# A relu-squared attention with a mixture of adapters behind it: the loads of A and B are planned behind q and k of the fourth and fifth quads

## The chip, the cores and the metric

The kernel runs on one core of one Trainium2 chip. The metric is the device time of one execution in microseconds; lower is better. Times are given as the median of several runs, and one execution is profiled.

## The reference

Eight batches of twelve heads, 448 positions, head size 64. The attention has no softmax: the scores are clipped at zero and squared. Its output, 3584 rows of 768, goes through a gate that picks two of eight adapters of rank 16 for each row and adds what they give.

```python
scores = scale * np.matmul(q, k.transpose(0, 1, 3, 2))
attn = np.maximum(scores, 0.0) ** 2 / S
x = np.matmul(attn, v)            # then (B*S, H*D) = (3584, 768)
logits = x @ w_gate               # the two largest of 8 are kept
w = exp(sel - max); w /= w.sum()
for e in range(8):                # rows that picked e
    delta[mask] += w[mask] * ((x[mask] @ A[e]) @ B[e])
out = x + delta
```

q, k, v are float32 of 8x12x448x64; A is 8x768x16, B is 8x16x768.

## The kernel before

**Tiles.** Four heads of one batch are loaded together; this is called a quad here, and there are 24 (eight batches `b` with three quads `c` each), numbered from 0. One load of a quad's q, k or v is two DMAs from POOL (`load`, L337 to L355; L342 is its line in the profile), one for each half of the 128 partitions, and it casts float32 to bf16 on the way. The rings hold three quads of q, three of k and six of v. q of the first quad comes another way (SP and ACT), its k in two pieces (L362).

**Stages.** For a quad, TensorE transposes q and k (`tp`, 56 small matmuls, L496), and VectorE copies the result to `qkT` (L509). Then come seven steps `j`, each with a step index `n` that runs through the kernel: `qk` (L545, four matmuls into two PSUM banks), `relu` on ACT (L569; for the first seven steps VectorE may do it, L571), the square on VectorE for two steps at once (L588), and `pv` (L606). After seven steps the result is copied to `xt` (L629). Behind the attention, groups of three tiles of 128 rows go through the gate (L647 to L704), a transpose of the weighted z (L730, L744), and each tile then gets its output: x by an identity matmul (L761), the adapters' second product with `B_sb` in two groups of eight matmuls (L781), two copies out of PSUM (L805) and the stores from SP (L825).

**A, B and sel.** `a_raw` and `g_raw` hold A and the gate's weights as loaded by `aw_fn` (L404, L408). `sel`, made on POOL by a memset and a select (L392, L393), is the 0/1 matrix with which TensorE puts A's rows in order (`aw_place`, L424, 72 matmuls, copied at L434 to `awg`). The gate reads `awg`. `b_fn` (L412) loads B twice, once to each half of the partitions.

**Order.** Nothing is ordered by hand. Every piece of work is an `Op` with the engines it may run on, a duration and a latency in us, the pieces it depends on, and a rank. `schedule` (L68) plays them through on a clock of its own, gives each engine the ready piece with the smallest rank, and the program is then issued in the order of the planned starts. On the chip, each engine follows this fixed order and waits where data is missing; a planned dependency that stands for no data is no wait there. A load has duration 0.63 for each half and latency 2.5; users see it 0.05 later. Its rank is the number of the quad, plus 1.2 for v. `sel_op` and `a_load` have rank 3.5, `b_load` 4.5. The first loads (`first_load`) have no dependencies; a later load depends on the transposes of the quad three before, and from some point on it really waits for a given relu (`pace`). On TensorE, `pick` (L123) takes the smallest rank with a surcharge for changing the matmul mode, but turns to the next `qk` when the piece chosen would outlast what ACT still has before it:

```python
cover = max(free["ACT"], t) + sum(o.dur["ACT"] for o in relus)
if q and t + best.dur[e] + 0.1 * (best.mode != mode) + 0.1 * (best.mode != "64") + 0.4 > cover + SLACK:
    return q[0]
```

At most three pairs of PSUM banks may hold scores at a time (`SCAP`).

The functions that the diff touches:

Of the kernel before, what the change touches and what calls it, by code (L numbers as in the profile page):

```python
# [14 lines left out]
J = 7  # L15
# [18 lines left out]
E_O0 = 1  # L34
E_O1 = 0
E_Z = 1
SYNC = mybir.DependencyInfo(mybir.DependencyClass.Sync, mybir.DependencyReason.DATA)
LEAD = -10
LSTEP = 2.0
# [8 lines left out]
class Op:  # L48
    def __init__(
        self, engs, dur, lat, fn, deps=(), after=None, mode=None, kind="", take=(), give=(), rank=0.0,  # L50
        banks=None, free=(),
    ):
        self.engs, self.fn = engs, fn
        self.dur = dur if isinstance(dur, dict) else dict.fromkeys(engs, dur)
        self.lat = lat if isinstance(lat, dict) else dict.fromkeys(engs, lat)
        self.deps, self.mode, self.kind = [d for d in deps if d is not None], mode, kind
        self.after = after
        self.take, self.give, self.rank = take, give, rank
        self.want, self.free, self.banks = banks, free, None
        self.start = self.end = self.eng = None  # L60
        self.users = []
        self.missing = len(self.deps) + (after is not None)
        self.ready = 0.0
        for d in self.deps + [after] * (after is not None):
            d.users.append(self)


def schedule(ops, switch=0.1, hop=0.05):  # L68

    free = {e: 0.0 for o in ops for e in o.engs}  # L70
# [3 lines left out]
    used = {"s": 0, "t": 0, "p": 0, "m": 0, "o": 0, "z": 0}  # L74
    events, returns = [0.0], []
    mode = None
    relus, port = [], []
    qks = sum(o.kind == "qk" for o in ops)
    seq = {id(o): i for i, o in enumerate(ops)}
    for o in ops:  # L80
# [3 lines left out]
    t = 0.0  # L84
# [63 lines left out]
    while left:  # L148
        for r in [r for r in returns if r[0] <= t + 1e-9]:
            if r[1] == "bank":  # L150
                for x in r[2]:
                    freed[x] = r[0]
                used[r[3]] -= r[4]
            else:
                level[r[1]] += 1
            returns.remove(r)
        moved = False
        for e in free:
            if free[e] > t + 1e-9:
                continue  # L160
            o = pick(e)
            if o is None:
                continue
            st = t
            if e == "PE":
                if mode is not None and o.mode != mode:
                    st += switch
                mode = o.mode
            o.start, o.eng = st, e
            free[e] = st + o.dur[e]  # L170
            o.end = st + o.dur[e] + o.lat[e]
            if o.kind == "sq":
                port[:] = [free[e]]
            for x in o.engs:
                avail[x].remove(o)
            for p in o.take:
                level[p] -= 1
            if o.want is not None:
                o.banks = choose(o)
                for x in o.banks:  # L180
                    del freed[x]
                used[o.want[0]] += 1
            back = o.end + hop
            for p in o.give:
                returns.append((back, p))
            for owner, i in o.free:
                c = owner.want[0]
                two = c in "stz"
                returns.append((back, "bank", owner.banks if two else [owner.banks[i]], c,
                                0.5 if c in "po" else 1))  # L190
            events.append(back)
            for u in o.users:
                u.missing -= 1
                u.ready = max(u.ready, st if u.after is o else back)
                if not u.missing:
                    for x in u.engs:
                        avail[x].append(u)
                    events.append(u.ready)
                    if u.kind == "relu":
                        relus.append(u)  # L200
            if o.kind == "relu":
                relus.remove(o)
            events.append(free[e])
            qks -= o.kind == "qk"
            order.append(o)
            left -= 1
            moved = True
        if not moved:
            events = sorted(set(x for x in events if x > t + 1e-9))
            assert events, "the schedule is stuck"  # L210
            t = events[0]
# [12 lines left out]
def kernel(  # L224
# [98 lines left out]
    def both(o, w):  # L323

        return ps[:, o.banks[0] : o.banks[0] + 2, :].rearrange("p a x -> p (a x)")[:, 512 - w : 512 + w]

    PE, DVE, ACT, ANY = ("PE",), ("DVE",), ("ACT",), ("ACT", "DVE")
    DL, AL, PL = 0.084, 0.19, 0.165
    
# [7 lines left out]
    def load(b, w, c, deps, pace=()):  # L337

        def fn(g):
            if g == 0:  # L340
                T[b, w, c] = loads[w].tile([128, 2, J * Dh], BF16, name=f"{'qkv'[w]}n_{b}_{c}", tag="x")
            i = nc.gpsimd.dma_start(  # L342
                out=T[b, w, c][g * PH : g * PH + PH],
                in_=(qv, kv, vv)[w][b, g, :, 2 * c : 2 * c + 2, :],
            )
            if pace:
                tc.add_manual_dep(i.ins, relu_in[pace[g]].ins.name, SYNC, reason="loads keep step with the work")

        l = []
        for g in range(2):  # L350

            l.append(op(("POOL",), 0.63, 2.5, lambda g=g: fn(g), kind="load", after=l[-1] if l else None,
                        deps=(deps if not l else []) + ([relu_ops[pace[g]]] if pace else []),
                        rank=b * NC_ + c + (1.2 if w == 2 else 0.0)))
        return l  # L355
# [60 lines left out]
    def aw_place(half, deps):  # L416
# [21 lines left out]
        ms = []  # L438
        for x in range(3):
            ms.append(op(PE, 6 * 0.085, PL, lambda x=x: mm(x), deps=deps, after=ms[-1] if ms else None,  # L440
                         mode="128", kind="fill", banks=("m", 1) if x == 0 else None, rank=D_A))
        return op(DVE, dve(3 * ZW), DL, ev, deps=ms, free=[(ms[0], 0)], rank=D_A)


# [42 lines left out]
    def tp(b, c):  # L487
# [23 lines left out]
        units = [(w, j) for w in range(2) for j in range(J)]  # L511
        if not first:
            m = op(PE, 2 * TPD, PL, lambda: mm(units), deps=loaded[b, 0, c] + loaded[b, 1, c] + [ident_op],
                   mode="64", kind="tp", banks=("t", 2), take=("qkT",), rank=first_use[b, c] + D_TP)
            return op(DVE, dve(4 * J * PH, 1.92), DL, lambda: ev(nc.vector.tensor_copy, 0, 2 * J * PH),
                      deps=[m], free=[(m, 0)], rank=m.rank + D_TPE)
        m = op(PE, 0.26, PL, lambda: mm(units[: J + 1]), deps=loaded[0, 0, 0] + [k0_first, ident_op],
               mode="64", kind="tp", banks=("t", 2), take=("qkT",), rank=-30.0)
        m2 = op(PE, 0.2, PL, lambda: mm(units[J + 1 :]), deps=[loaded[0, 1, 0]], after=m, mode="64", rank=-30.0)
        n_ = (J + 1) * PH  # L520

        e = [
# [114 lines left out]
    def gate(tiles_):  # L637
# [4 lines left out]
        for t in range(n):  # L642

            def mm(t=t):
                z = bank(zops[0])
                for do in range(DO):
                    nc.tensor.matmul(  # L647
                        out=z[:, t * ZW : t * ZW + ZW],
                        lhsT=xt[:, do, 128 * tiles_[t] : 128 * tiles_[t] + 128],
                        rhs=awg[:, do, :],  # L650
                        start=(do == 0),
                        stop=(do == DO - 1),
                    )

            zops.append(op(PE, 0.355, PL, mm, mode="128", kind="fill", deps=aw_ops + [x for tl in tiles_ for x in xdeps[tl]],
                           after=zops[-1] if zops else None, banks=("m", 1) if t == 0 else None, take=("zp",) if t == 0 else (), rank=v + D_Z))

        def z3():
# [62 lines left out]
        for t in range(n):  # L721

            def f_zt(t=t):

                for k_ in range(2):
                    for c in range(2):
                        for h in range(2):
# [7 lines left out]
                                stop=True,  # L735
                            )

            zts.append(op(PE, 0.235, PL, f_zt, mode="64", kind="zt", deps=[o_zp],
                          after=zts[-1] if zts else None, banks=("z", 2) if t == 0 else None,
                          take=("zT",) if t == 0 else (), give=("zp",) if t == n - 1 else (), rank=v + D_ZT))  # L740

# [8 lines left out]
    def outputs(tile_):  # L750
# [5 lines left out]
        def f_id():  # L756
            for do in range(DO):
                for tok in range(2):
# [8 lines left out]
                            skip_group_check=True,  # L767
                        )

        o_id = op(PE, 0.2, PL, f_id, mode="64", kind="id", deps=[o_zT, b_load] + xdeps[tile_],  # L770
                  banks=("o", 2), take=("osb",), rank=v + D_ID)
        prev = o_id
        for k_ in range(2):
# [19 lines left out]
            if k_:  # L793
                zuse[g0] -= 1
                last = zuse[g0] == 0
            prev = op(PE, 0.69, PL, f_b, mode="64", kind="fill", deps=[o_id], after=prev,
                      give=("zT",) if last else (), rank=v + D_ID)

        evs = []
# [85 lines left out]
    for n, (b, u, c, j) in enumerate(order):  # L885
        if (b, c) not in seen:
# [3 lines left out]
            if b2 < B:  # L890
                old = divmod(b2 * NC_ + c2 - RING[2], NC_)
                for w in range(3):
                    x = n + LEAD + LSTEP * w
                    loaded[b2, w, c2] = load(b2, w, c2, [
                        tp_ops[b, c], pv_ops[last_use[old]] if w == 2 and old in last_use else None
                    ], pace=[int(x), int(x + LSTEP / 2)] if x + LSTEP < n and x > 0 else ())
            if (b, c) == (0, 2):
                b_load = op(("POOL",), 1.3, 3.0, b_fn, kind="load", rank=4.5)
        qk_ops[n] = qk(n)
        relu_ops[n] = relu(n)  # L900
        sq(n)
# [41 lines left out]
```

## Time and profile before

| | |
|---|---|
| median of 5 runs | 198.08 us (197.5 to 199.45) |
| profiled execution | 197.56 us |
| its span, first to last instruction | 195.7 us |
| granted TensorE clock | 0.999 |
| busy: PE / DVE / ACT / POOL | 165.6 / 166.7 / 164.9 / 90.9 us |
| DMA | 29.43 MB in 26941 packets, mean 150 GB/s |

A line of the profile names the kernel's line, the engine, the operation and the tiles, then how often and how long. Idle time stands with what ended it. A stretch gives the busy time of each engine in it; a chain follows back from the last instruction what released each step. POOL's DMA rows are the issue of a DMA, not its transfer; the transfer lands later.

### The profile page before, as it was taken

The numbers are of one execution on the slowest core, as the hardware profiler recorded it, in microseconds if no ns is written. First come the engines' busy times: TensorE is split into PE (matmuls) and PEld (weight loads), VectorE is DVE, ScalarE is ACT, GpSimd is POOL, SyncE is SP. The second block draws the span as 40 slices with busy tenths as digits, with TensorE's granted clock in tenths as the row PEclk, the third lists the DMA queues.
The fourth block names the chain that finished last, engine by engine and source line by source line (L and its number), as shares of the span: only waits on it lengthen the run. The fifth ranks groups of instructions, "written<-read, shape, count | busy, mean of one in ns | idle before, by whom it ended". The sixth has DMA issues, their size and how long they took to land.

```text
span 195.7 us, 10479 instructions
## 1 busy us (share of the span) xinstructions
PE 165.6 (85%) x4664; PEld 111.1 (57%) x4664; DVE 166.7 (85%) x292; ACT 164.9 (84%) x255; POOL 90.9 (46%) x156
## 2 busy tenths in 40 slices
PE   0678898679959899999986999899996899999990
PEld 0345365448635666576644675667564678766750
DVE  0399996999879899999998989998999998677550
ACT  3589987999959899999998999999999999664320
POOL 7989976998835455555374644464300000000000
PEclk9999999999999999999999999999999999999999
DMA  5998999999998999999999899999910326510775
GB/s 106 143 186 133 133 215 190 167 169 186 188 229 143 174 116 178 179 154 151 210 147 196 124 175 172 165 148 229 186 41 3 98 71 160 127 46 10 185 214 166
DMA packets 26941, 29.43 MB, mean 150 GB/s; under 512 B 4752, under 2 KB 23184, under 8 KB 26896
## 3 DMA queue, kind: packets, MB, share of 16 engines
q0 software_dynamic: 22080, 17.29, 64.5%
q1 hardware_dynamic: 4672, 11.24, 18.9%
q8 instruction: 36, 0.59, 1.3%
q10 hardware_dynamic: 144, 0.23, 0.4%
q14 instruction: 9, 0.07, 0.1%
HBM read 34.23 MB, written 11.01 MB: 231 GB/s over the span
## 4 chain that ended last, share of the span: by engine, by line
PE 37%; ACT 17%; DVE 16%; issue 11%; DMA 10%; POOL 7%; SPq 0%; POOLq 0%; ACTq 0%; DVEq 0%
ACT a L569 14%; PE ps L781 10%; PE ps L545 8%; DVE a L588 8%; DMA kn<-in_k_dram 8%; PE ps L606 7%; PE ps L496 3%; PE ps L647 3%; DMA out_dram<-osb 2%; PE ps L730 2%; POOL qn L342 2%; DVE osb L805 2%; PE ps L761 2%; DVE zT L744 1%; ACT xt L629 1%
## 5 line engine op out<-in xcount | busy, mean ns | idle before, releaser
L569 ACT ACTIVATE a<-ps 128x896 bf16<-128x896 f32 (+2 forms) x187 | 146.6, 879 | 11.7 <-PE ps L545 9.7
L588 DVE TENSOR_TENSOR a<-a 128x1792 bf16<-128x1792 bf16 (+3 forms) x96 | 92.1, 972 | 3.6 <-ACT a L569 3.2
L545 PE MATMUL ps<-qkT 64*64 64x448 bf16 (+2 forms) x756 | 70.8, 365 | 8.3 <-ACT a L569 6.4
L545 PEld LDWEIGHTS <-qkT 64*64 64x64 bf16 x756 | 30.5, 107 | 31.7 <-issue 21.0
L781 PE MATMUL ps<-B_sb,zT 64*64 64x384 f32 x448 | 46.7, 488 | 0.0
L606 PE MATMUL ps<-a,vn 64*64 64x448 bf16 (+2 forms) x756 | 45.4, 330 | 1.1 <-DMA a_raw<-in_moe_A_dram 0.4
L342 POOL DMA_DIRECT2D qn<-in_q_dram x46 | 27.6, 608 | 23.0 <-ACT a L569 18.0
L342 POOL DMA_DIRECT2D vn<-in_v_dram x48 | 28.9, 610 | 13.4 <-ACT a L569 8.4
L342 POOL DMA_DIRECT2D kn<-in_k_dram x46 | 27.6, 608 | 11.1 <-ACT a L569 7.4
L509 DVE COPY qkT<-ps 128x1792 bf16<-128x1792 bf16 (+2 forms) x25 | 25.9, 1037 | 6.7 <-PE ps L496 6.5
L606 PEld LDWEIGHTS <-vn 64*64 64x64 bf16 x756 | 25.8, 107 | 9.9 <-issue 3.7
L805 ACT COPY osb<-ps 128x384 f32<-128x384 f32 x28 | 14.9, 531 | 7.8 <-PE ps L781 7.8
L496 PE MATMUL ps<-identb,qn 64*64 64x64 bf16 x672 | 12.3, 200 | 10.4 <-DVE qn L379 5.7
L496 PEld LDWEIGHTS <-qn 64*64 64x64 bf16 x672 | 11.5, 114 | 16.2 <-issue 8.8
L781 PEld LDWEIGHTS ps<-B_sb,zT 64*64 64x64 f32 x448 | 18.2, 134 | 2.9 <-issue 1.2
L805 DVE COPY osb<-ps 128x384 f32<-128x384 f32 x28 | 15.5, 553 | 4.4 <-PE ps L781 4.4
L629 DVE CAST xt<-ps 128x448 bf16<-128x448 f32 (+2 forms) x28 | 16.4, 590 | 0.6 <-PE ps L606 0.2
L496 PE MATMUL ps<-identb,kn 64*64 64x64 bf16 x672 | 13.1, 199 | 3.7 <-DMA kn<-in_k_dram 1.6
L761 PEld LDWEIGHTS <-xt 64*64 64x64 bf16 x672 | 12.3, 109 | 4.1 <-issue 2.2
L629 ACT CAST xt<-ps 128x448 bf16<-128x448 f32 (+2 forms) x26 | 12.7, 496 | 1.8 <-PE ps L606 1.8
L647 PE MATMUL ps<-awg,xt 128*128 128x136 bf16 x168 | 13.6, 224 | 0.3
L647 PEld LDWEIGHTS <-xt 128*128 128x128 bf16 x168 | 10.0, 98 | 5.2 <-issue 4.9
(38 smaller groups left out, 96.7 us busy)
## 6 DMA issues: line engine op xcount, KB each, us to landing
out_dram<-osb SPq DMA_DIRECT2D x49, 192.0 KB, 4.2
vn<-in_v_dram POOLq DMA_DIRECT2D x48, 112.0 KB, 4.8
qn<-in_q_dram POOLq DMA_DIRECT2D x46, 112.0 KB, 4.4
kn<-in_k_dram POOLq DMA_DIRECT2D x46, 112.0 KB, 4.4
B_sb<-in_moe_B_dram POOLq DMA_DIRECT2D x2, 384.0 KB, 6.5
out_dram<-osb SPq DMA_DIRECT2D x5, 144.0 KB, 2.4
out_dram<-osb SPq DMA_DIRECT2D x1, 336.0 KB
q<-in_q_dram SPq DMA_DIRECT2D x1, 224.0 KB, 3.6
```

The costliest lines, as they stand in the source:

```text
L342: i = nc.gpsimd.dma_start(out=T[b, w, c][g * PH : g * PH + PH], in_=(qv, kv, vv)[w][b, g, :, 2 * c : 2 * c + 2, :],)
L496: nc.tensor.transpose(ps_b[sl * PH : sl * PH + PH, m.banks[g], (w * J + j) * PH : (w * J + j) * PH + PH,], T[b, w, c][r, sl, j * Dh : j * ...
L509: cp(T["qkT", b, c][:, g0:g1, x0:x1], ps_b[:, m.banks[0] + g0 : m.banks[0] + g1, x0:x1])
L545: nc.tensor.matmul(out=cols(bank(o, sl)[a * PH : a * PH + PH, x0 : x0 + W]), lhsT=qk_[r0 : r0 + PH, a, (J + j) * PH : (J + j) * PH + PH], ...
L569: relu_in[n] = nc.scalar.activation(T["a1", g0][:, i], both(qk_ops[n], W), ACTF.Relu, scale=relu_scale)
L588: (nc.gpsimd if n in pool_sq else nc.vector).tensor_mul(a2, T["a1", g0], T["a1", g0])
L606: nc.tensor.matmul(out=bank(head, g)[sl * PH : sl * PH + PH, :W], lhsT=vn[r0 : r0 + PH, sl, j * Dh : j * Dh + Dh], rhs=T["a2", g0][r0 : r0 ...
L629: evac(W, lambda cp, g=g: cp(xt[:, g * NC_ + c, col : col + W], bank(src, g)[:, :W]), engs=SETS[(E_X0, E_X1)[g]] if n < NS - FREE else ANY ...
L647: nc.tensor.matmul(out=z[:, t * ZW : t * ZW + ZW], lhsT=xt[:, do, 128 * tiles_[t] : 128 * tiles_[t] + 128], rhs=awg[:, do, :], start=(do = ...
L761: nc.tensor.matmul(out=bank(o_id, r)[tok * PH : tok * PH + PH, do * PH : do * PH + PH], lhsT=xt[rr, do, c0 + tok * PH : c0 + tok * PH + PH ...
L781: nc.tensor.matmul(out=bank(o_id, r)[tok * PH : tok * PH + PH, : D // 2].rearrange("p (o d) -> p o d", o=DO), lhsT=T["zT", g0][rr, tok, x0 ...
L805: cp(T["osb", tile_].rearrange("p (o r d) -> p r o d", r=2, d=PH)[:, r], bank(o_id, r)[:, : D // 2].rearrange("p (o d) -> p o d", o=DO),)
```

## The change

The diff adds planned dependencies: `sel_op` and `a_load` follow the second half of k of quad 3 (the fourth), `b_load` that of k of quad 4 (the fifth). It sets the planned duration of half a load from 0.63 to 0.70, and that of a group of eight matmuls with `B_sb` from 0.69 to 0.655. It also gives each piece on TensorE a number of matmuls `mm` and has the planner delay TensorE at each multiple of 128 matmuls by a time `FETCH` after the multiple before, and sets FETCH to 0.

```diff
+FETCH = 0.0
...
-            o.end = st + o.dur[e] + o.lat[e]
+            if e == "PE":
+
+                x = 128 - block[0] % 128
+                while x <= o.mm:
+                    at = free[e] - o.dur[e] * (1 - x / o.mm)
+                    free[e] += max(0.0, block[1] + FETCH - at)
+                    block[1] = max(at, block[1] + FETCH)
+                    x += 128
+                block[0] += o.mm
+            o.end = free[e] + o.lat[e]
...
+    def follow(o, d):
+        o.deps.append(d)
+        o.missing += 1
+        d.users.append(o)
+
...
-            l.append(op(("POOL",), 0.63, 2.5, lambda g=g: fn(g), kind="load", after=l[-1] if l else None,
+            l.append(op(("POOL",), 0.7, 2.5, lambda g=g: fn(g), kind="load", after=l[-1] if l else None,
...
-            prev = op(PE, 0.69, PL, f_b, mode="64", kind="fill", deps=[o_id], after=prev,
+            prev = op(PE, 0.655, PL, f_b, mode="64", kind="fill", mm=8, deps=[o_id], after=prev,
...
+            if (b, c) == (0, 0):
+                follow(sel_op, loaded[b2, 1, c2][1])
+                follow(a_load, loaded[b2, 1, c2][1])
             if (b, c) == (0, 2):
-                b_load = op(("POOL",), 1.3, 3.0, b_fn, kind="load", rank=4.5)
+                b_load = op(("POOL",), 1.3, 3.0, b_fn, deps=[loaded[1, 1, 1][1]], kind="load", rank=4.5)
```

The other lines of the diff hand `mm` to the pieces (4 by default, 12 for a third of `aw_place`, 56 for `tp`, and so on).

More of the change, by code (lines that the diff above doesn't have):

```diff
@@ L50, in __init__ @@
         self, engs, dur, lat, fn, deps=(), after=None, mode=None, kind="", take=(), give=(), rank=0.0,
-        banks=None, free=(),
+        banks=None, free=(), mm=4,
     ):
-        self.engs, self.fn = engs, fn
+        self.engs, self.fn, self.mm = engs, fn, mm
         self.dur = dur if isinstance(dur, dict) else dict.fromkeys(engs, dur)
@@ L76, in schedule @@
     mode = None
-    relus, port = [], []
+    relus, port, block = [], [], [33, -9.0]
     qks = sum(o.kind == "qk" for o in ops)
@@ L440, in aw_place @@
             ms.append(op(PE, 6 * 0.085, PL, lambda x=x: mm(x), deps=deps, after=ms[-1] if ms else None,
-                         mode="128", kind="fill", banks=("m", 1) if x == 0 else None, rank=D_A))
+                         mode="128", kind="fill", mm=12, banks=("m", 1) if x == 0 else None, rank=D_A))
         return op(DVE, dve(3 * ZW), DL, ev, deps=ms, free=[(ms[0], 0)], rank=D_A)
@@ L513, in tp @@
             m = op(PE, 2 * TPD, PL, lambda: mm(units), deps=loaded[b, 0, c] + loaded[b, 1, c] + [ident_op],
-                   mode="64", kind="tp", banks=("t", 2), take=("qkT",), rank=first_use[b, c] + D_TP)
+                   mode="64", kind="tp", mm=56, banks=("t", 2), take=("qkT",), rank=first_use[b, c] + D_TP)
             return op(DVE, dve(4 * J * PH, 1.92), DL, lambda: ev(nc.vector.tensor_copy, 0, 2 * J * PH),
@@ L517, in tp @@
         m = op(PE, 0.26, PL, lambda: mm(units[: J + 1]), deps=loaded[0, 0, 0] + [k0_first, ident_op],
-               mode="64", kind="tp", banks=("t", 2), take=("qkT",), rank=-30.0)
-        m2 = op(PE, 0.2, PL, lambda: mm(units[J + 1 :]), deps=[loaded[0, 1, 0]], after=m, mode="64", rank=-30.0)
+               mode="64", kind="tp", mm=32, banks=("t", 2), take=("qkT",), rank=-30.0)
+        m2 = op(PE, 0.2, PL, lambda: mm(units[J + 1 :]), deps=[loaded[0, 1, 0]], after=m, mode="64", mm=24, rank=-30.0)
         n_ = (J + 1) * PH
@@ L653, in mm @@
                     )
-            zops.append(op(PE, 0.355, PL, mm, mode="128", kind="fill", deps=aw_ops + [x for tl in tiles_ for x in xdeps[tl]],
+            zops.append(op(PE, 0.355, PL, mm, mode="128", kind="fill", mm=6, deps=aw_ops + [x for tl in tiles_ for x in xdeps[tl]],
                            after=zops[-1] if zops else None, banks=("m", 1) if t == 0 else None, take=("zp",) if t == 0 else (), rank=v + D_Z))
@@ L736, in f_zt @@
                             )
-            zts.append(op(PE, 0.235, PL, f_zt, mode="64", kind="zt", deps=[o_zp],
+            zts.append(op(PE, 0.235, PL, f_zt, mode="64", kind="zt", mm=16, deps=[o_zp],
                           after=zts[-1] if zts else None, banks=("z", 2) if t == 0 else None,
@@ L768, in f_id @@
                         )
-        o_id = op(PE, 0.2, PL, f_id, mode="64", kind="id", deps=[o_zT, b_load] + xdeps[tile_],
+        o_id = op(PE, 0.2, PL, f_id, mode="64", kind="id", mm=24, deps=[o_zT, b_load] + xdeps[tile_],
                   banks=("o", 2), take=("osb",), rank=v + D_ID)
```

## The prediction

> **What bounds the kernel now.** I read the busy shares first, then the stretches, then who waits for whom, then POOL's and PE's timelines where the change acts. The first two lines are ACT's and DVE's busy time in section 1 of the page; the next three are 20 us stretches (stretch, length, busy us of PE, PEld, DVE, ACT, POOL, then clock, DMA share, GB/s).
>
> ```profile
> PE 165.6 (85%) x4664; PEld 111.1 (57%) x4664; DVE 166.7 (85%) x292; ACT 164.9 (84%) x255; POOL 90.9 (46%) x156
> ...
> 15.00:35.00 20.00, 16.59 (x440) 10.34 (x438) 18.31 (x21) 18.06 (x23) 16.93 (x27) 1.00 1.09 169
> ...
> 55.00:75.00 20.00, 16.89 (x490) 11.44 (x494) 17.47 (x30) 17.20 (x25) 9.16 (x16) 1.00 0.98 167
> 75.00:95.00 20.00, 18.78 (x561) 12.37 (x556) 19.53 (x33) 19.98 (x29) 10.32 (x18) 1.00 1.00 167
> ```
>
> Three engines are equally loaded. From 75 to 95 us ACT is busy 19.98 of 20 and DVE 19.53: nothing can be won there. Time lost early is not caught up, so an early gap of ACT and DVE is worth its length at the end, until PE alone sets the tail after 160 us. Between 10 and 140 us ACT waits 4.9 us in seven waits on qk matmuls and 1.0 us once for a pv group, so this is about all that a better order can return before the tail. Where these waits lie, PE's and POOL's timelines show (start, length, operation, and in brackets the idle time before it with its releaser).
>
> ```profile
> 15.04 1.18 POOL L342 DMA_DIRECT2D vn<-in_v_dram  x2 [0.96 <-DMA kn<-in_k_dram]
> 16.20 0.77 POOL L392 MEMSET sel<- 128x773 bf16 x1
> 17.05 1.46 POOL L393 TENSOR_SCALAR_AFFINE_SELECT sel<-sel 128x773 bf16<-128x773 bf16 x1
> 18.46 0.91 POOL L404 DMA_DIRECT2D a_raw<-in_moe_A_dram  x1
> 19.36 0.56 POOL L408 DMA_DIRECT2D g_raw<-in_moe_w_gate_dram  x1
> 19.91 1.22 POOL L342 DMA_DIRECT2D qn<-in_q_dram  x2
> 21.09 1.23 POOL L342 DMA_DIRECT2D kn<-in_k_dram  x2
> 22.25 1.25 POOL L342 DMA_DIRECT2D vn<-in_v_dram  x2
> 23.42 1.30 POOL L412 DMA_DIRECT2D B_sb<-in_moe_B_dram  x2
> 24.65 1.27 POOL L342 DMA_DIRECT2D qn<-in_q_dram  x2
> 25.83 0.69 POOL L342 DMA_DIRECT2D kn<-in_k_dram  x1
> ```
> ```profile
> 31.91 0.41 PE L496 MATMUL ps<-identb,qn 64*64 64x64 bf16 x26 [0.32 <-DMA qn<-in_q_dram]
> 32.46 0.22 PE L496 MATMUL ps<-identb,kn 64*64 64x64 bf16 x2
> 33.04 0.41 PE L496 MATMUL ps<-identb,kn 64*64 64x64 bf16 x26 [0.36 <-DMA kn<-in_k_dram]
> ...
> 56.52 0.22 PE L496 MATMUL ps<-identb,qn 64*64 64x64 bf16 x3 [2.33 <-issue]
> ```
>
> Count quads from 0 by their q rows: q1 to q3 are out by 12.9 us, then follow k3, v2, sel, A, gate, q4, k4, v3, B, q5, k5. The fourth quad (3) is thus already ahead of A, and the fifth (4) already ahead of B. The transposes of quad 5 stand in PE's order before their data is there, and PE is stopped twice. Behind it ACT stands still 1.02 us before 33.88 and DVE 1.54 us before 33.56. Quad 4 costs ACT 0.30 and 0.47 us around 27 to 28.7, quad 6 another 0.30 before 37.96. Together 2.1 us of ACT. The largest single stop, 2.33 us, is not a load: PE stops after 25 of 28 transposes of one half of a tile, where no data boundary lies, and the releaser is "issue".
>
> **The change part by part.** No instruction is added or removed. `follow` and the new `deps` are edges of the planner alone; on the chip no wait comes with them, only another order. Inert: with FETCH at 0 the new loop adds max(0, earlier start − later start), which is 0, so `mm` and the block counter cost nothing, and there is no cover to lose.
>
> *POOL's order.* By the code, a load counts as landed 2.5 + 0.05 us after its issue, and the issue of a half goes from 0.63 to 0.70. In the plan k3 ends at 15.7, so sel and A may start at 18.25. Meanwhile POOL takes what is free: v2 to 17.1, then both halves of q4 to 18.5. Then sel and A (rank 3.5) go ahead of k4 (rank 4). The same happens to B: k4 ends at 23.6, B is free at 26.15; v3 goes to 25.0, q5 to 26.4, then B, then k5. So the new order is k3, v2, **q4**, sel, A, gate, k4, v3, **q5**, B, k5: only two q loads pass. With measured steps (a load 1.17, sel 2.26 from 16.20 to 18.46, A and gate 1.45, B 1.23) q4 goes out at 16.2 instead of 19.9, A at 19.6 instead of 18.5, q5 at 23.4 instead of 24.65, B at 24.6 instead of 23.4, and k4 and k5 at 21.1 and 25.8, where they are today. A quad is transposed when q and k have both landed; k sets it, so the moved DMAs themselves win 0. The bounds: a queue shorter by q4 when k4 is issued could give one load's step, 1.17 us, less the 1.17 by which A starts later, so about 0 to −0.3; and A's small pieces now stand directly ahead of k4, +0.2 at worst. I take −0.1. Behind k5 comes q6, which now waits 1.09 us before its first half at 30.04 and 0.94 before its second. The page names matmuls, on which q6 doesn't depend; the two B transfers, issued at 23.4 and 24.0 and landing 6.1 to 7.0 us later, fit. That wait passes to k6; k6 was issued at 32.44 and may gain or lose half a microsecond. A later is covered by the matmuls of L424 being filler (23.9 to 29.7) whose result is first used at 35.2; without this cover its 1.2 us would be on the path. B is first read at 47.4, so its 1.2 us are covered by some 16 us.
>
> *PE's order.* This is where I expect the effect. In the plan of before, k4 lands at 24.6 and k5 at 29.7; measured, quad 4's last transposes started at 26.68 and quad 5's at 33.04. In the new plan they land at 26.15 and 31.65. So transposes go into PE's fixed order 1.5 to 2 us later, behind one or two more qk and pv groups, while the real landings stay. Quad 5 is needed only at the relu with index 35, by the count of ACT's rows at 39.7, some 5 us after its qkT copy ends, so later costs nothing; the stop moves behind work for ACT. Of the 1.02 us at quad 5 I take 0.9, of the 1.07 at quads 4 and 6 I take 0.4. Bounds: 0 (if ACT has no finished qk at that point, since at most three groups of banks run ahead) and 2.1. Sum −1.3.
>
> The Trainium skill (DMA: Bandwidth & Descriptors, Anatomy of one DMA — SWDGE path) fits a DMA to about 2.0 us plus bytes over 436 GB/s. That would be an estimated 2.3 us for 112 KB, near the plan's 2.5, and by it k5 would have been early and this term 0. The page's section 6 has 4.4 us for these loads, and the stop at 33.04 shows it; I go by the row.
>
> *Filler price.* 56 groups of L781 go from 0.69 to 0.655 in the plan; the chain's pieces of eight are 0.63 to 0.69. They take what they took: 0 directly. But everything behind is planned anew. Nothing shown prices a new plan as a whole; the nearest rows bound it: of ACT's 4.9 us on qk, 4.1 lie before 60 us (0.80, 0.30, 0.47, 0.30, 2.22), so 0.8 are left to win from 60 to 140, and to lose there are 56 places at up to 0.3 us (the commonest short gap in these rows), of which a quarter would be 4.2. I take 0.
>
> *The stop at 54 us.* Queue 8 moved 36 packets and 0.59 MB, that is 16 KB at a time, and the 10479 instructions are mostly PE's. I read the stop as PE waiting for its next block of instructions behind a full DMA. Its place depends on how many transposes, which are quick to run through, share a block, and on loads then waiting. A new order shifts both. Bounds −2.2 (ACT's share of it gone) to +2.2 (a second one). Such a stop is the only one over 1.1 us in this trace, so a new order is likelier to lose it than to double it; I take −0.6.
>
> The Trainium skill (Runtime: NRT & Kernel Launch, Instruction fetch mechanics) says blocks of 16 KiB are fetched ahead and crossing one is mostly hidden. The size agrees with queue 8; the 2.33 us do not look hidden, and by the page this term would be 0 and the sum 0.6 us longer.
>
> Sum: −0.1 − 1.3 + 0 − 0.6 = −2.0. The profiled execution took 197.56 us (span 195.7 and 1.9 around it), so 195.6; the median of the five runs, 198.08, stands 0.5 above it. I forecast **196.0**, against the median.
>
> **The rivals.** *Only q moves* (198.0, chance 0.28, within 1%): k lands when it lands, PE stops as today at another group, and the stop at 54 us stays. For it: k4 and k5 keep their issue times. Against it: 5 us of room for quad 5's transposes. It also covers the case that the change doesn't do what it says, since A and B already stand behind the quads named.
>
> *Fillers ahead of qk* (201.0, chance 0.32, slower): the planner calls qk when a filler's price would outlast ACT's cover. At 0.035 us less, an L781 group is let in where qk was called before. Place: 60 to 150 us, where ACT is 98% busy and has no reserve. Price: 0.3 us of ACT per miss; 14 of 56 give +4.2, less 1.3 won early, 198.08 + 2.9 = 201.0. It decides from 11 misses on (3.3 less 1.3 is 2.0, about 1%). For it: the order of before leaves ACT almost no wait there, so a changed one can hardly be better. Against: the pieces of eight measure 0.65, so the new price is truer.
>
> *Stop gone wholly and quads won wholly* (194.0): −2.2 and −2.1. It belongs to the forecast's side.
>
> **How the numbers follow.** Forecast and its better edge 0.40; only q moves 0.28; fillers 0.32. These are also the chances of faster by over 1% (under 196.1), within 1%, and slower by over 1% (over 200.1); 1% is about what runs of 197.5 to 199.45 can tell from no change. The likeliest case's own range is 193.8 (4.3 us won) to 196.1. The range that should hold 8 in 10 goes from 193.6 to 201.6: the upper end holds the filler case up to 16 misses.
>
> **What would show it.** Right: POOL issues q4 before sel and q5 before B; ACT has no gap over 0.5 us from 26 to 40; the index 35 relu comes about 1 us earlier; no PE stop by issue over 1.1 us. Wrong: k4 or k5 issued ahead of A or B (the plan read wrongly); ACT's waits on qk between 60 and 140 us over 2 us (fillers); gaps before 40 us unchanged.

## Result and the profile after

| | before | changed |
|---|---|---|
| median | 198.16 us (71 runs, 194.91 to 202.89) | 198.68 us (38 runs, 195.95 to 203.27) |
| ratio | 1 | 1.0065, 95% interval 1.0039 to 1.0091 |
| ratio, measured again later (12 runs, beside 35 of before) | 1 | 0.9999, interval 0.9958 to 1.0040 |

By the first ratio the change costs 1.3 us (0.8 to 1.8 us), by the second nothing; a gain of 2 us was forecast. The ratios compare undisturbed runs alone, and the first profile of the changed kernel is of a disturbed one (202.16 us, span 200.4), so the stages below are read from its second profile, of the run called after_again (span 195.6).

The line of section 1 of the page, and the stretches that answer to those shown of before (stretch, length, busy us of PE, PEld, DVE, ACT, POOL, clock, DMA share, GB/s), of the first profile:

```profile
PE 169.0 (84%) x4664; PEld 111.8 (56%) x4664; DVE 165.8 (83%) x290; ACT 166.0 (83%) x257; POOL 91.1 (45%) x156
...
15.00:35.00 20.00, 17.18 (x455) 11.36 (x456) 18.81 (x22) 18.18 (x22) 16.14 (x25) 0.91 1.09 168
...
55.00:75.00 20.00, 16.68 (x483) 11.30 (x478) 18.68 (x30) 18.33 (x27) 10.80 (x19) 1.00 1.03 178
75.00:95.00 20.00, 18.11 (x530) 11.81 (x526) 18.18 (x31) 19.26 (x29) 9.47 (x16) 1.00 0.97 164
```

The three engines are as evenly loaded as before. POOL's timeline (start, length, operation) of the same profile has the order that was worked out, q of quad 4 ahead of sel and q of quad 5 ahead of B:

```profile
16.19 1.18 POOL L357 DMA_DIRECT2D qn<-in_q_dram  x2
17.35 0.77 POOL L407 MEMSET sel<- 128x773 bf16 x1
18.20 1.58 POOL L408 TENSOR_SCALAR_AFFINE_SELECT sel<-sel 128x773 bf16<-128x773 bf16 x1
19.73 0.91 POOL L419 DMA_DIRECT2D a_raw<-in_moe_A_dram  x1
...
21.19 1.22 POOL L357 DMA_DIRECT2D kn<-in_k_dram  x2
22.36 1.23 POOL L357 DMA_DIRECT2D vn<-in_v_dram  x2
23.53 1.25 POOL L357 DMA_DIRECT2D qn<-in_q_dram  x2
24.69 1.30 POOL L427 DMA_DIRECT2D B_sb<-in_moe_B_dram  x2
27.62 1.21 POOL L357 DMA_DIRECT2D kn<-in_k_dram  x2 [1.63 <-DMA kn<-in_k_dram]
```

k of quad 4 is issued at 21.19, where it was at 21.09. k of quad 5 does not keep its place: it waits 1.63 us here and goes out at 27.62; in the second profile it goes out at 26.36, against 25.83 before.

The transposes of quad 5 on PE's timeline, which lost 0.32 and 0.36 us to DMA before, now look like this (second profile):

```profile
33.91 0.39 PE L511 MATMUL ps<-identb,qn 64*64 64x64 bf16 x28
34.13 0.36 PE L511 MATMUL ps<-identb,kn 64*64 64x64 bf16 x23
35.66 0.25 PE L511 MATMUL ps<-identb,kn 64*64 64x64 bf16 x5 [1.16 <-issue]
```

They stand two microseconds later and no longer wait for a load. But PE stops 1.16 us by "issue" after 23 of the 28 transposes of k, and ACT waits for it as it did before:

```profile
24.74 0.92 ACT L584 ACTIVATE a<-ps 128x896 bf16<-128x896 f32 x1 [0.45 <-PE ps L560]
25.99 5.02 ACT L584 ACTIVATE a<-ps 128x896 bf16<-128x896 f32 x6 [0.34 <-PE ps L560]
31.33 3.58 ACT L584 ACTIVATE a<-ps 128x896 bf16<-128x896 f32 x4 [0.32 <-PE ps L560]
36.13 0.92 ACT L584 ACTIVATE a<-ps 128x896 bf16<-128x896 f32 x1 [1.22 <-PE ps L560]
```

These four gaps of ACT make 2.33 us; the four of before made 2.09. Single profiles differ by more than that: ACT's gaps over 0.2 us from relu 20 to relu 37 make 2.09, 3.07, 1.90 and 2.85 us in four profiles of before's plan (some are of runs described below) and 1.70, 2.33 and 1.51 in three of the changed one. On the mean the change saves 0.6 us here, of the 1.3 forecast.

Now the run behind its first 25 us, in three stages, cut where the relus with index 21, 91 and 133 start. First before (its first profile), then the changed kernel (second profile):

```profile
25.16:95.13 69.97, 60.72 (x1802) 41.38 (x1801) 64.76 (x102) 65.00 (x91) 43.95 (x75) 1.00 1.07 177
95.13:135.65 40.52, 36.84 (x1057) 24.64 (x1047) 38.88 (x62) 39.35 (x57) 21.86 (x37) 1.00 0.99 166
135.65:195.69 60.04, 52.36 (x1458) 36.11 (x1450) 45.84 (x110) 41.86 (x86) 2.36 (x4) 1.00 0.45 113
```
```profile
25.99:92.99 67.00, 58.39 (x1711) 39.09 (x1707) 63.86 (x100) 63.93 (x89) 43.88 (x74) 1.00 1.07 179
92.99:132.99 40.00, 37.47 (x1096) 25.47 (x1090) 39.22 (x64) 39.83 (x59) 21.90 (x37) 1.00 1.01 173
132.99:195.60 62.61, 54.55 (x1504) 37.52 (x1496) 45.44 (x108) 42.50 (x89) 2.41 (x5) 0.98 0.45 111
```

These six lines hold the main part of the answer. From relu 21 to 91 the changed kernel is 2.97 us quicker. But PE does 91 matmuls fewer in that stage (1711 for 1802), 2.33 us less work; it stands idle 8.6 us (67.00 less 58.39) where it stood 9.2. Of the lead, only 0.6 us is idle time saved. Of the 91 matmuls 85 come back: 39 in the middle stage and 46 in the last, which is 2.57 us longer with 2.19 us more of PE's work and almost the same idle time (8.1 for 7.7).

### The profile page after: what moved, and what is told of

Same layout as the page of the kernel before. It is cut to its first block, busy times and chain, and to the rows that moved or that the text cites. A ratio compares the mean times of both kernels' runs of the same rounds, so it can differ in the third digit from the quotient of the medians.

```text
span 200.4 us, 10485 instructions
## 1 busy us (share of the span) xinstructions
PE 169.0 (84%) x4664; PEld 111.8 (56%) x4664; DVE 165.8 (83%) x290; ACT 166.0 (83%) x257; POOL 91.1 (45%) x156
## 5 line engine op out<-in xcount | busy, mean ns | idle before, releaser
L621 PE MATMUL ps<-a,vn 64*64 64x448 bf16 (+2 forms) x756 | 47.1, 340 | 1.9 <-issue 1.3
L621 PEld LDWEIGHTS <-vn 64*64 64x64 bf16 x756 | 24.9, 109 | 12.3 <-issue 5.2
L820 ACT COPY osb<-ps 128x384 f32<-128x384 f32 x28 | 14.3, 511 | 9.6 <-PE ps L796 6.8
L511 PE MATMUL ps<-identb,qn 64*64 64x64 bf16 x672 | 11.7, 198 | 8.7 <-DVE qn L394 5.7
L662 PE MATMUL ps<-awg,xt 128*128 128x136 bf16 x168 | 14.1, 233 | 1.7 <-issue 1.7
L662 PEld LDWEIGHTS <-xt 128*128 128x128 bf16 x168 | 10.8, 102 | 6.3 <-issue 6.1
L511 PE MATMUL ps<-identb,kn 64*64 64x64 bf16 x672 | 12.4, 199 | 2.1 <-issue 1.6
```

The lines of the kernel that those rows point to most:

```text
L511: nc.tensor.transpose(ps_b[sl * PH : sl * PH + PH, m.banks[g], (w * J + j) * PH : (w * J + j) * PH + PH,], T[b, w, c][r, sl, j * Dh : j * ...
L621: nc.tensor.matmul(out=bank(head, g)[sl * PH : sl * PH + PH, :W], lhsT=vn[r0 : r0 + PH, sl, j * Dh : j * Dh + Dh], rhs=T["a2", g0][r0 : r0 ...
L662: nc.tensor.matmul(out=z[:, t * ZW : t * ZW + ZW], lhsT=xt[:, do, 128 * tiles_[t] : 128 * tiles_[t] + 128], rhs=awg[:, do, :], start=(do = ...
L820: cp(T["osb", tile_].rearrange("p (o r d) -> p r o d", r=2, d=PH)[:, r], bank(o_id, r)[:, : D // 2].rearrange("p (o d) -> p o d", o=DO),)
```

## Experiments

Each run's ratio is to before on the same chip. "Before's plan" is the order of PE, DVE and ACT of before, "the changed plan" that of the changed kernel.

**The load order alone.** Both q loads are moved by hand in the finished order; nothing else changes.

```diff
-    for o in schedule(ops):
+    plan = schedule(ops)
+    for load_, x in ((loaded[1, 0, 1], sel_op), (loaded[1, 0, 2], b_load)):
+        for o in load_:
+            plan.remove(o)
+        i = plan.index(x)
+        plan[i:i] = load_
+    for o in plan:
```

> Before with POOL's order of the changed kernel and nothing else: q of quad 4 issued ahead of sel and A, q of quad 5 ahead of B; PE, ACT and DVE keep the order of before. Theory 1 (the new order on PE, ACT and DVE makes the difference): ratio 0.998 to 1.002, relu 35 within 0.3 us of before. Theory 2 (A, B and k being pushed behind q makes it): the loss of the change shows here, ratio 1.004 or more, with k of quad 5 issued over 1 us later.

> Before with POOL's order of the changed kernel, once more, since six runs gave 0.9895 with an interval of nearly a per cent. Theory 1 (load order does nothing that can be seen): 0.996 to 1.004. Rival: 0.986 to 0.994 again.

Measured: 0.9895 (0.9809 to 0.9981) with six runs, then 1.0029 (0.9981 to 1.0076) with twelve. The second, with twice the runs, does not bear the gain of the first out: the load order alone does nothing that can be seen. Relu 35 came at 40.47 us in the first profile of it, 0.8 later than in before's, where 0.3 had been allowed; in four profiles of before's plan it comes at 39.7 to 41.2 us, so that says nothing.

**The three planned figures, one by one.**

```diff
 edges_only: the changed kernel with both prices put back
-... op(("POOL",), 0.7, 2.5, ...     -... op(PE, 0.655, PL, f_b, ...
+... op(("POOL",), 0.63, 2.5, ...    +... op(PE, 0.69, PL, f_b, ...
 load_price_only: before with 0.7 for half a load
 filler_price_only: before with 0.655 for an L781 group
 edges_load: the changed kernel with 0.69 for an L781 group
```

> The changed kernel with both prices put back (half a load 0.63, an L781 group 0.69): the planned dependencies alone. Theory 1: PE gets its transposes of quads 4 and 5 later; a lead of about 1 us at relu 70 over before, as the changed kernel has (73.77 against 75.50), and part of it at the end: ratio 0.990 to 1.000. Rival (any new plan loses what the old one's tuned constants had): ratio 1.004 to 1.012 with no lead at relu 70.

> Before with half a load planned at 0.70 instead of 0.63 and nothing else. Theory 1: this too plans transposes later, a lead of 0.5 to 1.5 us at relu 70, ratio 0.990 to 1.002. Rival (any new plan loses): ratio 1.004 to 1.012.

> Before with an L781 group planned at 0.655 instead of 0.69 and nothing else. Theory 1: fillers are let in ahead of qk from 50 us on; no lead at relu 35, ACT's waits on qk from 60 to 150 us grow by 1 to 3 us, ratio 1.005 to 1.015. Rival (the price is truer and nothing is lost by it): ratio 0.995 to 1.002, the loss then lies in the load's price or the edges.

> The changed kernel with the price of an L781 group put back to 0.69. Theory T (the truer price moves the last zT transposes behind a whole tile's products, so that PE waits in the tail): 0.4 to 1.0 us better than the changed kernel, ratio to before 0.997 to 1.003, and no wait for zT in the last 10 us. Rival (the price is innocent): like the changed kernel, 1.003 to 1.009.

Measured: edges 1.0011 (0.9948 to 1.0073), load price 0.9863 (0.9784 to 0.9943), filler price 0.9925 (0.9874 to 0.9976), edges with load price 0.9889 (0.9832 to 0.9946). The medians of all runs say otherwise for two of them: edges 199.94 against 197.81 of before beside it, edges with load price 200.24 against 199.45. The load price and the filler price alone came out faster than either of their theories had it. But they were measured beside the same 23 runs of before as the 0.9895 above, and not again; whether either is a gain stays open.

The number of matmuls from relu 21 to 91 hardly scatters, and it tells which edit puts work off: 1802 to 1814 in four profiles of before's plan, 1822 with the load price, 1763 with the filler price, 1708 and 1706 with the two that have the edges, 1706 to 1711 with all three (the changed kernel twice and pool_order_back). By relu 91, 128 matmuls with `B_sb` have run in before's plan and with either price alone, and 112 in every plan with the edges, a tile's output less; by relu 147 it is 240 in all of them. So the added dependencies put off most of the work.

The stage from relu 147 to the last matmul, when no load is left, does not scatter as long as nothing is put ahead of the first quad: 41.8, 41.8, 41.7 and 41.7 us in four profiles of before's plan, 41.7 with the load price, 42.6 with the filler price, 42.9 and 42.9 with the two that have the edges, 43.4, 43.1 and 43.1 with all three. In this stage the load price is innocent, and the edges (1.1 us) and the filler price (0.9) each have a hand; together they make 1.4. Of the edges' 1.1 some 0.4 is one stop of PE by "issue", 0.56 us between two weight loads in both profiles and 0.09 to 0.16 at that place in before's plan. Of the filler price's 0.9, 0.42 is PE's wait for zT: it stands in the last 10 us of every plan with the filler price but after_tail, and in none without it; so far theory T is right. ACT's waits on qk from 60 to 150 us were 3.3 us with the filler price alone, inside the 0.8 to 6.2 of four profiles of before's plan: the expected growth is not shown.

**Both kernels again.**

> The kernel before, unchanged, to see what belongs to one execution and what to the plan. Theory A (the stops of PE for its next instructions and the half-clock stretches fall differently in each execution): ratio 0.994 to 1.006; the stop of 2.33 us at 54 us is shorter than 1.2 us or gone, other stops at the same places modulo 128 matmuls. Rival (the stop at 54 us belongs to this plan): it stands again within 1 us of 54 us and over 1.5 us long.

> The changed kernel, unchanged. Theory A: the long stop at 139.6 us and the half clock behind it are not there again; the lead over before at relu 70 (1.7 us in the first profile) is again 0.5 to 1.7, and the end lies 0 to 1 us behind before because of the tail, where PE waits for zT (0.42 us). Rival: the loss from relu 133 to 147 (3.5 us) is in the plan and stands again.

Measured: 0.9977 (0.9928 to 1.0025) and 0.9999 (0.9958 to 1.0040). The long stop of before is there again, at the same three transposes of the same quad, so the rival is right on that stop: its place belongs to the plan (it comes 1.8 us later on the clock, as the work ahead of it does). Its length varies; 0.46 us in pool_order_only (before's plan too), and in the profiles of before_again and of pool_order_again (also before's plan):

```profile
58.59 0.22 PE L496 MATMUL ps<-identb,qn 64*64 64x64 bf16 x3 [2.60 <-issue]
```
```profile
55.99 0.22 PE L496 MATMUL ps<-identb,qn 64*64 64x64 bf16 x3 [1.27 <-issue]
```

The changed kernel's loss from relu 133 to 147 (17.3 us in its first profile, 13.1 in before's) was for the greater part not the plan's: it takes 14.6 in the second. In the first profile PE stopped 1.70 us by "issue" in it, until 141.5 us, and the granted clock went to half for 3.4 us:

```profile
140.00:145.00 5.00, 3.46 (x33) 2.36 (x37) 2.66 (x6) 2.12 (x3) 0.00 (x0) 0.66 0.53 117
```

In the second, PE stops at the same matmul for 1.01 us, and the clock stays full there. The lead over before's first profile at relu 70 is 2.8 us in the second, more than the 1.7 expected at most. The wait for zT in the tail, 0.42 us, stood again.

**The changed plan with the old load order.** q of quads 4 and 5 is moved back, as above but to just before k of the same quad.

> The changed kernel with POOL's order of before (sel, A and gate ahead of q of quad 4, B ahead of q of quad 5); PE, ACT and DVE as changed. Theory 1 (PE's order decides, not the loads'): within 0.3% of the changed kernel, ratio 1.002 to 1.010. Rival (the load order gives something, as 0.9895 for it alone says): 0.5 to 1% slower than the changed kernel, ratio 1.010 to 1.016.

Measured: 0.9999 (0.9959 to 1.0038), like the changed kernel beside it (0.9999). POOL's order adds nothing that can be seen in the changed plan either.

**Fillers earlier in the tail.** PACE2 is the planned distance in steps between the due times of two tiles in the second half.

```diff
-    PACE2 = 5.565
+    PACE2 = 5.2
```

> The changed kernel with PACE2 at 5.2 instead of 5.565: tiles of the second half are due earlier; TensorE's order is the changed one up to about step 130, and behind it one tile's output and the last zT transposes stand earlier. Theory P (TensorE's total work and its idle time set the end; a filler moved earlier is no gain): the stretch from relu 133 to the last matmul, 57.4 to 57.7 us in the undisturbed changed plans and 54.5 to 55.8 in those of before, falls by 0.3 to 0.6 only, the wait for zT; ratio 0.2 to 0.3% below the changed kernel. Rival (filler left for the tail is the whole cost): it falls by 1.4 or more, ratio 0.7% below the changed kernel.

Measured: 1.0329 (1.0268 to 1.0391), and 64.0 us from relu 133 to the last matmul, 6.3 more where both theories expected less. Both missed. PE's timeline at the end shows why:

```profile
186.03 0.93 PE L745 MATMUL ps<-identf,zp 64*64 64x64 f32 x48 [2.13 <-DVE zp L719]
188.04 2.84 PE L796 MATMUL ps<-B_sb,zT 64*64 64x384 f32 x16 [0.89 <-DVE zT L759]
```

The last tiles go through gate, zp, transpose, zT and output one after the other. With their fillers done early nothing is left to stand beside this chain: PE waits 2.13 and 0.89 us, and the next group takes 2.84 us instead of some 1.5, with half the clock granted for 3.4 us from 187.5. Filler left for the tail is not a loss in itself; it is the cover of the last gate. The changed kernel lacks a little of it at the end; its last products, in the first profile:

```profile
193.92 1.52 PE L796 MATMUL ps<-B_sb,zT 64*64 64x384 f32 x16 [0.42 <-ACT zT L759]
```

**Moving the blocks.** Transposes of the identity are put ahead of the first quad, while PE waits for q, so that all later work stands 32, 64 or 96 matmuls further on.

```diff
+    def front():
+        for i in range(64):
+            r = slice((i % 2) * PH, (i % 2) * PH + PH)
+            nc.tensor.transpose(ps_b[:PH, 6 + i % 2, :PH], identb[r, r], identb[r, r])
+
     for o in schedule(ops):
         o.fn()
+        if o is ident_op:
+            front()
```

> Before with 64 transposes of the identity on TensorE ahead of the first quad, while it waits for q (idle until 5.74 us); their result is overwritten. Theory F (TensorE's stops by issue fall where a block of 128 matmuls ends): the stops, until now at matmul 95 modulo 128, stand at 31 modulo 128, so the stop at 54 us is somewhere else, and the time stays: 0.994 to 1.006. Rival (the stops belong to what is done there, a load or a wait): they stay at the same transposes.

> Before with POOL's order of the changed kernel and the 64 transposes ahead. If TensorE is busy earlier and its first half-clock stretch falls into the wait for q, relu 14 comes at 19.5 us or sooner (18.9 to 21.1 without): ratio 0.990 to 1.000. Rival: the front does nothing for the clock, the same as the load order alone.

> Before with 32 transposes of the identity ahead of the first quad. Theory S (where a block of 128 matmuls ends in the plan decides how long TensorE stands by issue): the stop of 2.3 to 2.6 us in the transposes of quad 9 is gone, all stops together differ from the 3.9 to 9.4 us of before's plan and the 9.8 and 10.1 with 64 ahead; the time moves with them, somewhere from 0.990 to 1.010. Rival (the 1.007 with 64 ahead comes from the work put in front): 1.003 to 1.006 here.

> Before with 96 transposes of the identity ahead. Theory S: as with 32, its own sum of stops and a time that goes with it, 0.990 to 1.010. Rival (work put in front costs): 1.008 to 1.012.

> The changed kernel with 32 transposes of the identity ahead. Theory S: stops of 5 to 10 us in all as without, at other work; ratio to before 0.993 to 1.013. The stage from relu 21 to 91 again 66 to 69 us against 67 to 73 in before's plan, and from relu 133 to the last matmul again 57 to 58 against 54 to 56: time is put off, not won. Rival (the stops decide the difference between the plans): a front that halves them brings the changed kernel under 0.992.

> The changed kernel with 96 transposes of the identity ahead; theories as with 32: 57 to 58 us from relu 133 to the last matmul and 66 to 69 from relu 21 to 91 by the theory of work put off; ratio 0.993 to 1.013.

Measured: before with 64 ahead 1.0070 (1.0028 to 1.0112), with 32 1.0125 (1.0062 to 1.0188), with 96 1.0251 (1.0165 to 1.0338); with the load order and 64 0.9966 (0.9918 to 1.0013); the changed kernel with 32 1.0005 (0.9939 to 1.0070). With 96 the changed kernel has no ratio on record: six runs from 197.86 to 205.51, median 201.81, against 198.48 of before beside it.

PE's idle times over 0.43 us that end by "issue" all stand before matmul 95 modulo 128, counted from 0 at the program's first, in every profile, with and without a front. Counted by the work, as the expectation did, they have thus moved by the front: the stop in quad 9's transposes is gone with each front, and others stand elsewhere, as with 96 ahead

```profile
58.91 0.57 PE L545 MATMUL ps<-qkT 64*64 64x448 bf16 x7 [3.12 <-issue]
```

The pauses at that place can be added up, from the start of one weight load to that of the next, each counted above 0.15 us if it is over 0.43. They make 5.8, 9.4, 3.9 and 7.4 us in four profiles of before's plan and 9.8, 10.1, 10.2 and 10.4 with a front; 8.4, 5.0 and 6.0 with the changed plan, 5.9 and 4.8 with a front on it. So the alignment moves the stops, and every front that was tried on before's plan gave more of them. That the stops make the time is not shown: with the load order and 64 ahead they make 10.1 us at a ratio of 0.9966, and the changed kernel with 96 ahead has a median 1.7% above before's, though they make 4.8 in its profile (197.86 us, its fastest run). A cost of the work put in front is not ruled out either, though 32 ahead (1.0125) costs before no less than 64 (1.0070). With 64 ahead the stage from relu 147 to the last matmul is 42.4 us, and 42.7 with the load order too, against 41.6 with 32 or 96: one block end there makes a pause of 0.77 and 1.04 us. With the load order and 64 ahead relu 14 came at 19.59 us, where 19.5 or sooner was expected of a gain, and the ratio is that of no change.

The stages stand in all of these. From relu 21 to 91: 67.5 to 73.6 us in eight profiles of before's plan (mean 70.7), 67.0 to 68.6 in five of the changed one (67.8). From relu 133 to the end of the span: 59.3 to 61.6 (60.4), and 61.9 to 63.4 (62.5) in the changed one without its first profile. On the mean the changed plan wins 2.9 us early and gives back 2.0 late, with other alignments and load orders among the profiles. From relu 133 to the last matmul the two fronts on the changed plan took 56.7 us, a little under the 57 to 58 expected.

## Why the prediction was wrong

*What it had right.* POOL's order and the issue of k of quad 4; that what effect there is comes by PE's order; that quad 5's transposes would stand about 2 us later and wait for no load; by the code, that `mm` and FETCH do nothing; that A and B, later, cost nothing that can be seen. Index 35's relu came at 39.1 and 40.2 us, against 39.7 and 41.2 in two profiles of before; that fits the 1 us forecast, but a single profile scatters by more. Of the other signs of being right two failed: ACT has gaps of 0.60 and 1.22 us between 26 and 40 us in the two profiles of the changed kernel, and PE stops by "issue" over 1.1 us are there (1.70 and 1.16 us in the first, 1.16 in the second). k of quad 5 did not keep its place either (27.62 and 26.36 us for 25.83). The time lies in the range, and within 1% of before had been given 0.28; but the forecast was faster.

*The step that failed first* is the sentence "an early gap of ACT and DVE is worth its length at the end, until PE alone sets the tail". It priced gains at ACT. The span is PE's work, 165.6 us in before, and its idle time, with the 5 us after its last matmul. The matmuls are the same 4664 in both plans, so an early lead of ACT counts only by what PE's idle time loses. From relu 21 to 91 PE's idle time was 9.2, 11.2, 6.6 and 9.4 us in four profiles of before's plan and 9.5, 8.6, 8.8, 9.5 and 8.5 in the changed one, means of 9.1 and 9.0. The lead was work put off, and the later stages took it back: from relu 133 to the end PE is busy 54.5 us in four profiles of the changed plan, 51.9 to 53.3 in eight of before's.

*The term −1.3.* Its mechanism was right, the transposes moved and the waits for loads went; its size was not. The gaps it was to remove (2.09 us of ACT) measured 2.33 after in the profile shown, and by the means above 0.6 us less. The load's wait at quad 5 was replaced by a stop by "issue" at the same transposes, 0.53 us in the first profile and 1.16 in the second. Its place belongs to the changed plan's alignment: in both it stands before weight load 607, four blocks of 128 and 95. That is the first rival's shape ("PE stops as today"), with another cause than the one it named.

*The term −0.6.* "Likelier to lose it than to double it" took one long stop for an outlier. The sum of the stops at the block ends was 3.9 to 9.4 us in before's plan and 5.0 to 8.4 in the changed one without a front: no gain shows there.

*The term 0 for the new plan* hid +1.4 us from relu 147 to the last matmul, in seven profiles without a front that hardly scatter. The filler rival named another place: fillers let in ahead of qk from 60 to 150 us. But by relu 91 fewer matmuls with `B_sb` had run than before (112 for 128), and ACT's waits on qk from 60 to 140 us, 2.5 and 1.6 us in the two profiles of the changed kernel, lie inside the 0.6 to 4.9 of before's plan.

*What stays open.* The stage sums leave the changed kernel 0.9 us ahead (2.9 less 2.0), the runs put it between level and 1.3 us behind. A profile is one execution, and in before's plan the early stage alone spreads over 6 us. That the added dependencies put work off is shown by the counts; why the planner does so was not tried.

## What to carry to other kernels

When several engines are equally loaded, price a saving by the idle time of the engine that works last, stage by stage, with the number of its instructions beside it: a stage that is quicker with fewer instructions has put work off, not won time. A wait that is removed from a fixed order is only gone if nothing else stops at that place. Where single runs spread by 4%, six runs can show a gain of 1%, with an interval clear of none, that twelve do not show again.

## What the hardware showed beyond that

TensorE stops by "issue" at many kinds of work (transposes, qk, pv, gate, products with `B_sb`). Every such stop over 0.43 us, in all profiles, stands at the same place modulo 128 matmuls; the longest is 3.12 us, and together the pauses there make 4 to 10 us of a run. Queue 8 had shown 36 packets of 16 KB, and 4664 matmuls are 36.4 times 128. That these stops are waits for instructions from that queue is inferred from the spacing and the number, not shown by a run that empties the queue.

The granted clock fell to half for 3.4 us, ahead of the last few us, in 10 of 18 profiles, at different times: at 15, 22, 37, 60, 141, 147 or 187.5 us. In four of them it did so no more than 1.5 us after a stop by "issue" of 1.26, 1.70, 2.60 or 3.12 us had ended; behind the stop of 2.33 us in before's first profile it did not. Whether a stop brings it on was not tried.
